# Talking-heads attention and Fourier mixing on one core: scores a step sooner, a fourth buffer of gathered rows, sums of weights in place

## The chip, the core and the metric

The program runs on one core of a Trainium2 chip. The metric is the device time of one execution in microseconds (us). Engines are named as the profile names them: PE is the matmul engine (TensorE), PEld its weight loads, DVE the vector engine, ACT the scalar engine, POOL the GpSimd engine, SP the engine that here only issues transfers.

## What is computed

Two blocks follow each other. The first is attention whose heads are mixed twice, before and after the softmax (8 batches, 12 heads, 448 rows, head width 64):

```
scores = scale * np.matmul(q, k.transpose(0, 1, 3, 2))
scores = np.einsum('bhij,hg->bgij', scores, w_pre)
attn = softmax of scores over j
attn = np.einsum('bhij,hg->bgij', attn, w_post)
x    = np.matmul(attn, v), heads side by side: (8, 448, 768)
```

The second adds to x the real part of a two-dimensional Fourier transform over rows and columns, normalizes, and applies two matrix products with a ReLU between them:

```
u  = x + np.real(np.fft.fft(np.fft.fft(x, axis=1), axis=2))
un = (u - mu) / np.sqrt(var + 1e-06)
out = u + np.maximum(un @ w_ch1, 0.0) @ w_ch2
```

All numbers are 32-bit floats, but the two weight matrices arrive as 64-bit floats and are turned into 32-bit ones in the kernel, piece by piece.

## The kernel before, in words

The kernel has two stages. `mix_phase` is the mixing stage: attention and the Fourier transform, batch by batch. `ffn_phase` is the matrix products, in which each block product is done by a scheme of seven products, so that the weights are needed as seven blocks: four pieces and three sums of pieces (and one piece is overwritten by a sum).

**Steps of the mixing stage.** Head mixing sums over heads, which lie in different products, so the rows must be regrouped. The scores of a block of 28 to 60 query rows go to an SBUF tile `Sb`; the rows of `Sb` that belong to one step (20 query rows, all 12 heads) are gathered by four DMAs into a tile `Kr`, in which heads lie along partitions. A batch has 8 blocks and `GS` = 23 steps, the stage 184 steps. The loop at its end goes over steps `s` and emits, in an order written out by hand in `ORDERS` (one list for even, one for odd steps):

- `pre` (L639): the premix, a matmul of `Kr` with the expanded `w_pre`, for step s + LM, LM = 2;
- `max0`, `max1` (L646, DVE), `exp0`, `exp1` (L653, ACT) and `scale` (L660 to L663, DVE and POOL) for step s + 2: the softmax, in tile `PP`;
- `post` (L673): the postmix for step s, and `turn` (L686, DVE), its transpose into `Pv`;
- `gather` (L628, issued by SP): the four DMAs for step s + LG, LG = 4;
- `conv`: one dealt operation of the weights' conversion;
- `QK`, `AV`, `full`: fillers, which are due at a step by the tables below.

PE, DVE, ACT and POOL execute in exactly the order in which the loop emits (`manual_schedule`). SP takes its transfers in program order and waits, before each one, for what it reads and for the place it writes.

**Fillers and their tables.** A table gives the step within a batch. `AT_T`: transposes of q and k (L585, copies at L474) for the next batch, for three pairs of heads. `AT_L`, `AT_V`: loads of q, k and v from POOL. `AT_QK`: score products of a block and a pair of heads (`emit_qk`, L611), counted from 7 steps ahead of the block's first step. `AT_AV`: attention times v (L703). `AT_X`: the transposes (L747) that begin the Fourier part; POOL then folds rows and columns (`fold`, L768 to L789), one or two folds per step (one in a step with loads of q or k). `AT_Z`: first Fourier product (`emit_z`, L812), four per batch, with a copy `z` on ACT. `AT_S`: second one (`emit_s2`, L828), four per batch, each followed by four additions on DVE (L839, L841); after the second of a pair the rows are stored, one tile by SP (L860) and one by POOL (L851). A step of 23 or more lies in the next batch's steps: 39 is its step 16.

**Copies behind products.** A filler's products go to one of four PSUM tiles `ms`; the copies out of it are kept in `pend` and emitted at the next `flush`.

**Buffers.** `Sb` has two buffers, `Kr` three, `PP` three. A gather for step T thus writes over the rows of step T - 3.

**Weights.** `_Weights.deal` hands out the conversion, one operation on DVE per step here: seven per piece (`begin` to `whole`) and four sums (`total`, L295). Pieces and sums have a tile each, named after the block's number (`wst0` to `wst6`), one buffer apiece; POOL stores them to memory (L235) and loads pieces (L227). A store is kept in `later` and issued at the start of the next deal. The mixing stage converts five groups of four pieces.

Of the kernel before, what the change touches and what calls it, by code (L numbers as in the profile page):

```python
# [10 lines left out]
F32 = mybir.dt.float32  # L11
U32 = mybir.dt.uint32
ALU = mybir.AluOpType
# [3 lines left out]
P = 128  # L17
# [68 lines left out]

AT_T = ((5, 9), (15, 17), (13, 15))
AT_L = ((-4, -3), (-2, -1), (0, 1), (2, 7), (11, 12), (13, 14))  # L90
AT_V = ((2, 3), (4, 5), (6, 7))
AT_QK = ((0, 2, 1), (0, 1, 2), (0, 1, 2), (1, 2, 2),
         (0, 1, 2), (0, 1, 2), (0, 1, 2), (0, 1, 2))
AT_AV = ((1, 2, 4), (0, 1, 3), (1, 3, 5), (1, 2, 4))
AT_X = ((13, 0), (23, 1), (28, 3), (29, 2))
AT_Z = (39, 39, 42, 42)
AT_S = ((40, 44), (46, 49))

ORDERS = tuple(o.split() for o in (
    "pre post flush AV max0 exp0 "  # L100
# [65 lines left out]
class _Weights:  # L166
# [12 lines left out]
        self.ops, self.pieces, self.raws, self.later = [], [], {}, []  # L179
        self.pre = []  # L180

    def open(self, ctx, tc, ahead=1, split=False):
        self.ahead, self.split = ahead, split

        def pool(name, bufs):
            return ctx.enter_context(tc.tile_pool(name=name, bufs=bufs,
                                                  reuse_waits="tile"))
        self.praw, self.ptmp = pool("wraw", ahead + 1), pool("wtmp", 1)
        self.pst = pool("wst", 1 + split)
# [24 lines left out]
    def add(self, c, n):  # L214

        nc, vec = self.nc, self.nc.vector
        ps, sums, w, dst = self._parts(c)[n]
        box, k0 = {}, len(self.pieces)
        self.pieces.extend(ps)

        def load(n):

            for k in range(len(self.raws), min(n + 1, len(self.pieces))):
                src, f, _ = self.pieces[k]
                raw = self.raws[k] = self.praw.tile([P, DH, 2], U32, name="raw64",
                                                    tag="raw64")
                self.eng.dma_start(out=raw[:, :f, :].rearrange("p f w -> p (f w)"),  # L227
                                   in_=src.bitcast(U32))

        def new(slot):  # L230
            box[slot] = self.pst.tile([P, DH], F32, name="wst", tag=f"wst{slot}")[:, :w]
            return box[slot]

        def store(slot):
            self.later.append(lambda: self.eng.dma_start(out=dst[slot], in_=box[slot]))  # L235

        def size(eng, hi, tmp):
            eng.tensor_scalar(tmp.bitcast(U32), hi, 0x7fffffff, None,
                              op0=ALU.bitwise_and)

        def clamp(eng, tmp):
            eng.tensor_scalar(tmp, tmp, _f32(0x38000000), _f32(0x47efffff),  # L246
                              op0=ALU.max, op1=ALU.min)

        def shift(eng, tmp, top):
            eng.tensor_scalar(top.bitcast(U32), tmp.bitcast(U32), 0x07ffffff, 3,  # L250
                              op0=ALU.bitwise_and, op1=ALU.logical_shift_left)

        def early(k):
            _, f, slot = ps[k]
            top = new(slot)
            tops.append(top)
            nc.scalar.activation(top, self.raws[k0 + k][:, :f, 1].bitcast(F32), ACTF.Abs)  # L257
            clamp(nc.gpsimd, top)

        def begin(k):  # L260
            _, f, slot = ps[k]
            load(k0 + k + self.ahead)
            raw = self.raws[k0 + k]
            box["lo"], box["hi"] = raw[:, :f, 0], raw[:, :f, 1]
            box["tmp"] = self.ptmp.tile([P, DH], F32, name="tmp", tag="tmp")[:, :f]
            box["slot"] = slot
            if self.split:
                while self.pre and self.pre[0][0] <= k0 + k + 2:
                    self.pre.pop(0)[1]()
                box["top"] = tops[k]  # L270
            else:
                box["top"] = new(slot)
                size(vec, box["hi"], box["tmp"])

        def sign():
            top = box["top"].bitcast(U32)
            vec.scalar_tensor_tensor(top, box["hi"], 0xc0000000, top,
                                     op0=ALU.bitwise_and, op1=ALU.bitwise_or)

        def power():  # L280
            vec.tensor_scalar(box["tmp"].bitcast(U32), box["top"].bitcast(U32),
                              0xff800000, None, op0=ALU.bitwise_and)

        def lower():
            vec.scalar_tensor_tensor(box["tmp"], box["lo"], 2.0 ** -52, box["tmp"],
                                     op0=ALU.mult, op1=ALU.mult)

        def whole():
            vec.tensor_tensor(box["top"], box["top"], box["tmp"], op=ALU.add)
            if box["slot"] != 6:  # L290
                store(box["slot"])

        def total(o, a, op, b):
            to = box[o] if o == 6 else new(o)
            vec.tensor_tensor(to, box[a], box[b], op=op)  # L295
            store(o)

        tops = []
        if self.split:
            self.pre.extend((k0 + k, lambda k=k: early(k)) for k in range(len(ps)))  # L300
        self.ops.append((lambda: load(k0 + self.ahead - 1), False))
        for k in range(len(ps)):
            self.ops.append((lambda k=k: begin(k), not self.split))
            if not self.split:
                self.ops.append((lambda: clamp(vec, box["tmp"]), True))
            self.ops.append((lambda: shift(vec, box["top" if self.split else "tmp"],
                                           box["top"]), True))
            for fn in (sign, power, lower, whole):
                self.ops.append((fn, True))
        for a in sums:  # L310
            self.ops.append((lambda a=a: total(*a), True))
# [124 lines left out]
def mix_phase(ctx, tc, rest, ident, q, k, v, w_pre, w_post, u_scr, u_rev, wts, lead):  # L436
# [13 lines left out]

    praw, pqt = lead.praw, lead.pqt
    psb = pool("psb", 2)
    pkr = pool("pkr", 3)
    ppp = pool("ppp", 3)
    psm = pool("psm", 4)
    cst = pool("cst")
    wts.open(ctx, tc)
    pvv = pool("pvv")
    ppv = pool("ppv", 2)
    pxt = pool("pxt", 2)  # L460
# [407 lines left out]
    def due(kind, at, fn):  # L868
        fill[kind].append((at, len(fill[kind]), fn))

    LG, LM = 4, 2
    for n in range(NK + FM):
        wts.add(0, n)
    for b in range(B):
        f = b * GS
        at_t = [(a, nm, xx) for xx, at in enumerate(AT_T) for nm, a in zip("qk", at)]
        if b == 0:

            for i, xx in enumerate(START):
                for j, nm in enumerate("kq"):  # L880
                    for y in range(2):
                        due("none", -40, lambda xx=xx, nm=nm, y=y: emit_load_qk(0, xx, nm, y))
                    due("full", 2 * i + j - 20, lambda xx=xx, nm=nm: emit_xpose(0, xx, nm))
                for n in range(2):
                    due("QK", 2 * i + 2 + n - 20, lambda n=n, xx=xx: (emit_qk(n, xx), n))
            for pr in range(3):
                for y in range(2):
                    due("none", -40, lambda pr=pr, y=y: emit_load_v(0, pr, y))
        else:
            for at, (a, nm, xx) in zip(AT_L, sorted(at_t, key=lambda e: e[0])):  # L890
                for y in range(2):
                    due("none", f + at[y] - GS,
                        lambda b=b, xx=xx, nm=nm, y=y: emit_load_qk(b, xx, nm, y))
            for xx, at in enumerate(AT_T):
                for nm, a in zip("qk", at):
                    due("full", f + a - GS,
                        lambda b=b, xx=xx, nm=nm: emit_xpose(b, xx, nm))
        for pr in range(3 if b else 0):
            for y in range(2):
                due("none", f + AT_V[pr][y], lambda b=b, pr=pr, y=y: emit_load_v(b, pr, y))  # L900
        for n in range(0 if b else 2, NBL):
            for xx in range(3):
                due("QK", f + BLOCK_AT[n] - 7 + AT_QK[n][xx],
                    lambda n=NBL * b + n, xx=xx: (emit_qk(n, xx), n))
        for n in range(NG):
            for pr in range(3):
                due("AV", f + GROUP_AT[n + 1] + AT_AV[n][pr],
                    lambda a=b * NG + n, pr=pr: (emit_av(a, pr), None))
            at, gi = AT_X[n]
            if b == B - 1 and n > 1:  # L910
                at += 2
            due("full", f + at, lambda g=groups[b * NG + gi]: emit_x(g))
        for n, at in enumerate(AT_Z):
            due("full", f + at, lambda b=b, n=n: emit_z(b, n // 2, n % 2))
        for pair in range(2):
            for par in range(2):
                due("full", f + AT_S[pair][par],
                    lambda b=b, pair=pair, par=par: emit_s2(b, pair, par))
# [607 lines left out]
```

## Time and profile before

| | us |
|---|---|
| median of three runs | 2340.01 |
| lowest and highest run | 2327.96, 2340.38 |
| the profiled execution | 2333.72 |
| its span (first to last instruction) | 2332.0 |
| first premix begins | 31.85 |
| last premix (step 183) begins | 800.00 |
| PE busy in the span | 2272.2 |

The span is what the profile covers; the profiled execution's own time holds 1.7 us around it. A line of the groups shows busy time and the mean of one instruction, then the idle time of the engine before it, and what ended it. A line of the waits reads: engine, tile and line, then what it waited for, then us in total, times, longest. `issue` means that nothing the profile shows was waited for. In the timeline each line has its start, its length, engine, line, tiles, shape, count, and in brackets the engine's idle time before it.

### The profile page before, as it was taken

How to read it: one execution, taken by the hardware profiler on the slowest of the kernel's cores; microseconds unless marked ns; L12 is line 12 of the kernel's file. 1: busy time of each engine (PE TensorE's matmuls, PEld its weight loads, DVE VectorE, ACT ScalarE, POOL GpSimd, SP SyncE). 2: the span in 40 equal slices, each digit the busy share in tenths (PEclk: the TensorE clock that was granted, in tenths of full speed). 3: DMA queues.
4: the chain of work that ended last, by engine and by line, in shares of the span. 5: the costliest groups of instructions: out<-in, count | busy, mean ns of one | idle time of the engine just before them, and what ended most of it. 6: DMA issues, size and time to landing. Idle time of an engine off the chain costs nothing.

```text
span 2332.0 us, 60769 instructions
## 1 busy us (share of the span) xinstructions
PE 2272.2 (97%) x22894; PEld 1752.2 (75%) x22894; DVE 1704.3 (73%) x3629; ACT 1176.3 (50%) x3336; POOL 1279.8 (55%) x1783
## 2 busy tenths in 40 slices
PE   6999999999999999999999999999999999999998
PEld 2445555555555567677899999999999899999998
DVE  3768877787877756787677787777777777856445
ACT  4676767666676622322354444444444445444434
POOL 3587977879777542121545455545545645444333
PEclk9999999999999999999999999999999999999999
DMA  7565665656656476567777887878877977795663
GB/s 163 153 178 167 184 180 153 193 170 185 183 170 190 142 229 217 183 219 272 204 178 209 209 227 203 213 175 253 210 166 196 287 166 183 193 249 113 148 148 68
DMA packets 231920, 439.04 MB, mean 188 GB/s; under 512 B 39624, under 2 KB 154080, under 8 KB 231630
## 3 DMA queue, kind: packets, MB, share of 16 engines
q1 hardware_dynamic: 158318, 303.56, 37.8%
q0 software_dynamic: 67312, 129.64, 29.7%
q8 instruction: 183, 3.00, 0.5%
q10 hardware_dynamic: 6000, 1.97, 0.5%
q14 instruction: 107, 0.88, 0.1%
HBM read 213.16 MB, written 142.76 MB: 153 GB/s over the span
## 4 chain that ended last, share of the span: by engine, by line
PE 88%; DMA 4%; DVE 3%; ACT 2%; SPq 1%; issue 1%; POOL 0%; ACTq 0%; DVEq 0%; POOLq 0%
PE psP L1192 18%; PE psP L1310 13%; PE psR L1192 9%; PE mx L639 7%; PE psR L1310 7%; PE ms L703 6%; PE ms L611 6%; PE po L673 5%; PE psQ L1192 5%; PE psQ L1310 3%; PE psP L1269 3%; DMA Kr<-Sb 3%; PE ms L828 2%; PE ms L585 1%; PE psR L1269 1%; PE ms L812 1%
## 5 line engine op out<-in xcount | busy, mean ns | idle before, releaser
L1344 POOL DMA_DIRECT2D out_dram<-od x171 | 207.8, 1275 | 261.3 <-DVE od L1332 167.9
L663 POOL TENSOR_SCALAR PP<-PP,rcp 128x448 f32<-128x448 f32 x368 | 236.9, 653 | 203.3 <-DVE rcp L661 170.2
L653 ACT ACTIVATE PP<-mx,nmx 128x448 f32<-128x448 f32 x368 | 230.6, 631 | 188.3 <-DVE nmx L646 170.7
L646 DVE TENSOR_REDUCE nmx<-mx 128x1 f32<-128x448 f32 x368 | 214.1, 619 | 133.1 <-PE mx L639 129.9
L1156 POOL TENSOR_TENSOR hq<-h 128x128 f32<-128x128 f32 (+1 forms) x210 | 128.1, 610 | 262.9 <-ACT h L1214 127.6
L1338 ACT COPY od<-psP 128x192 f32<-128x192 f32 x488 | 156.4, 321 | 182.0 <-PE psP L1310 177.5
L1341 DVE TENSOR_TENSOR od<-od 128x768 f32<-128x768 f32 x211 | 201.7, 969 | 53.9 <-ACT od L1338 52.9
L639 PE MATMUL mx<-Kr,kw 60*32 60x448 f32 x2944 | 217.4, 551 | 9.1 <-DMA Kr<-Sb 8.5
L611 PE MATMUL ms<-kT,qT 64*32 64x448 f32 (+1 forms) x3072 | 205.9, 545 | 8.1 <-ACT qT L474 6.3
L686 DVE STREAM_TRANSPOSE Pv<-po 128x896 f32<-128x896 f32 x184 | 203.8, 1108 | 5.2 <-PE po L673 2.6
L474 ACT COPY Sb<-ms 124x448 f32<-124x448 f32 (+1 forms) x384 | 184.6, 540 | 37.3 <-PE ms L611 24.5
L673 PE MATMUL po<-PP,kw 60*32 60x448 f32 x2944 | 197.2, 539 | 1.0 <-issue 1.0
L703 PEld LDWEIGHTS ms<-Pv,vv 64*64 64x64 f32 x5376 | 137.3, 132 | 70.9 <-issue 54.3
L1192 PE MATMUL psP<-ks,w1t 128*128 128x256 f32 x744 | 179.1, 379 | 0.1
L1192 PE MATMUL psP<-qs,w1t 128*128 128x256 f32 x744 | 179.0, 379 | 0.0
L703 PE MATMUL ms<-Pv,vv 64*64 64x120 f32 (+1 forms) x5376 | 159.6, 263 | 0.9 <-issue 0.9
L246 POOL TENSOR_SCALAR wst<-wst 128x256 f32<-128x256 f32 (+1 forms) x76 | 119.0, 1574 | 67.7 <-ACT wst L257 66.4
L1192 PEld LDWEIGHTS psP<-ks,w1t 128*128 128x128 f32 x744 | 139.4, 190 | 16.7 <-DVE u L1274 0.7
L1192 PEld LDWEIGHTS psP<-qs,w1t 128*128 128x128 f32 x744 | 139.5, 190 | 16.5 <-issue 0.2
L1310 PE MATMUL psP<-wt,h 128*128 128x192 f32 x490 | 120.8, 328 | 11.7 <-DVE od L1332 11.7
L1192 PE MATMUL psP<-ub,w1t 128*128 128x256 f32 x528 | 127.0, 379 | 0.0
L1213 DVE TENSOR_TENSOR h<-h,psP 128x512 f32<-128x512 f32 x42 | 28.8, 687 | 130.2 <-PE psP L1192 112.7
(190 smaller groups left out, 5294.6 us busy)
## 6 DMA issues: line engine op xcount, KB each, us to landing
Kr<-Sb SPq DMA_DIRECT2D x736, 105.0 KB
out_dram<-od POOLq DMA_DIRECT2D x171, 384.0 KB, 6.8
qs<-ub SPq DMA_DIRECT2D x89, 384.0 KB
ks<-ub SPq DMA_DIRECT2D x88, 384.0 KB
ub<-ub SPq DMA_DIRECT2D x79, 384.0 KB
w1t<-w SPq DMA_DIRECT2D x42, 384.0 KB
w2t<-w SPq DMA_DIRECT2D x42, 384.0 KB
raw<-in_moe_w_ch_dram SPq DMA_DIRECT2D x32, 384.0 KB
```

The costliest lines, as they stand in the source:

```text
L611: nc.tensor.matmul(pss[x][o:o + hi - lo, :S], st["qT", xx][64 * x:64 * x + 64, y, lo:hi], st["kT", xx][64 * x:64 * x + 64, y, :], start=Tr ...
L639: nc.tensor.matmul(mx[x][64 * z + o:64 * z + o + 32, :S], kw1[64 * x:64 * x + KR, o:o + 32], Kr[64 * x:64 * x + KR, z, :], start=True, sto ...
L646: nc.vector.tensor_reduce(nmx[:, :], steps[T]["mx"][x][:, :S], axis=AX.X, op=ALU.max, negate=True)
L653: nc.scalar.activation(steps[T]["PP"][:, x, :], steps[T]["mx"][x][:, :S], ACTF.Exp, bias=steps[T]["nmx", x][:, :], accum_out=steps[T]["den ...
L663: nc.gpsimd.tensor_scalar(PP[:, x, :], PP[:, x, :], rcp[:, x:x + 1], 1.0, op0=ALU.mult, op1=ALU.mult)
L673: nc.tensor.matmul(po[o:o + 32, z, :S], kw2[64 * z:64 * z + KR, y, :], PP[64 * z:64 * z + KR, :, c * HS:(c + 1) * HS], start=True, stop=True)
L686: nc.vector.transpose(turned[a]["Pv"][:, j, :].rearrange("p (z s) -> p z s", z=2), steps[T]["po"][:, :, :S])
L703: nc.tensor.matmul(pss[y][64 * x:64 * x + 64, :nu * R], st["v", pr][64 * y:64 * y + 64, x, jb * D:(jb + 1) * D], _ap(Pv, 64 * y * rp + 32 ...
L1192: mm = nc.tensor.matmul(p[:, m, :], w1[i][:, kc, m * P:(m + 1) * P], ub[:, kc, :], start=i in (0, 4, 1)[:3 - seed] and m == kc == 0, stop= ...
L1310: nc.tensor.matmul(ps[j, key][:, :DQ], a, b, start=m in (0, 4), stop=True, skip_group_check=True)
L1341: eng.tensor_tensor(D[j][:, :, :], D[j][:, :, :], D[k][:, :, :], op=ALU.add)
L1344: nc.gpsimd.dma_start(out=acc[t, r, d], in_=D[j][:, :, :], accum_op=ALU.add)
```

## The change

Four things are edited, all in the mixing stage.

- `LG` goes from 4 to 5: a step's rows are gathered one step sooner. The score products come one step sooner as well (counted from 8 steps ahead). `Kr` has four buffers instead of three.
- The tables follow: transposes of k for the second pair at 16 instead of 17; the last four loads of q and k a step sooner; one product of attention and v a step later.
- Fourier steps: the second Z goes from 39 to 40, the third from 42 to 40; S moves from 40 to 42 for the first pair's first half, and from 49 to 48 for the second pair's second half.
- The weights' sums are written in place of a piece that is no longer needed (`tight`), so that four tiles serve in place of seven; pieces and sums are taken in another order for it. The matrix-product stage opens its weights without this, as before.

```
-AT_T = ((5, 9), (15, 17), (13, 15))
-AT_L = ((-4, -3), (-2, -1), (0, 1), (2, 7), (11, 12), (13, 14))
+AT_T = ((5, 9), (15, 16), (13, 15))
+AT_L = ((-4, -3), (-2, -1), (0, 1), (2, 7), (10, 11), (12, 13))
...
-AT_AV = ((1, 2, 4), (0, 1, 3), (1, 3, 5), (1, 2, 4))
+AT_AV = ((1, 2, 4), (0, 1, 3), (1, 3, 5), (1, 3, 4))
...
-AT_Z = (39, 39, 42, 42)
-AT_S = ((40, 44), (46, 49))
+AT_Z = (39, 40, 40, 42)
+AT_S = ((42, 44), (46, 48))
...
+        tight = self.tight
+        if tight:
+            if ps[3][2] == 3:
+                ps = ps[3:] + ps[:3]
+            sums = [sums[x] for x in (0, 2, 1, 3)]
...
         def new(slot):
-            box[slot] = self.pst.tile([P, DH], F32, name="wst", tag=f"wst{slot}")[:, :w]
+            tag = [p[2] for p in ps].index(slot) if tight else slot
+            box[slot] = self.pst.tile([P, DH], F32, name="wst", tag=f"wst{tag}")[:, :w]
...
         def total(o, a, op, b):
-            to = box[o] if o == 6 else new(o)
+            if o == 6:
+                to = box[o]
+            elif tight:
+                to = box[o] = box[{(4, ALU.add): 3, (4, ALU.subtract): 0, (2, ALU.subtract): 1,
+                                   (3, ALU.subtract): 1}.get((o, op), ps[3][2] if n >= NK
+                                                             else 0)]
+            else:
+                to = new(o)
...
-    pkr = pool("pkr", 3)
+    pkr = pool("pkr", 4)
...
-    wts.open(ctx, tc)
+    wts.open(ctx, tc, tight=True)
...
-    LG, LM = 4, 2
+    LG, LM = 5, 2
...
-                due("QK", f + BLOCK_AT[n] - 7 + AT_QK[n][xx],
+                due("QK", f + BLOCK_AT[n] - 8 + AT_QK[n][xx],
```

More of the change, by code (lines that the diff above doesn't have):

```diff
@@ L180, in __init__, with open @@
         self.pre = []
-    def open(self, ctx, tc, ahead=1, split=False):
-        self.ahead, self.split = ahead, split
+    def open(self, ctx, tc, ahead=1, split=False, tight=False):
+        self.ahead, self.split, self.tight = ahead, split, tight
         def pool(name, bufs):
```

## The prediction

> **What bounds the kernel now.** I read the page first. Its slices of the span (the kernel has two stages; the mixing stage fills the first fourteen of the forty slices) show TensorE busy nearly everywhere, at full clock:
>
> ```profile
> PE 2272.2 (97%) x22894; PEld 1752.2 (75%) x22894; DVE 1704.3 (73%) x3629; ACT 1176.3 (50%) x3336; POOL 1279.8 (55%) x1783
> ...
> PE   6999999999999999999999999999999999999998
> ...
> PEclk9999999999999999999999999999999999999999
> ```
>
> No other engine is above 73% and the chain that ended last is 88% PE. So only PE's own stalls are worth time. The change touches the mixing stage alone, so I then asked for busy times from 64 us (after the start-up) to 803 us (after the last step):
>
> ```profile
> 64.00:803.00 739.00, 724.89 (x14496) 390.70 (x14482) 581.19 (x1219) 509.88 (x1569) 565.42 (x877) 1.00 0.58 173
> ```
>
> The columns are length, then busy PE, PEld, DVE, ACT, POOL, then granted clock, DMA share and GB/s. PE looks idle for only 14.1 us, but ends of matmuls are modelled, so a stall can hide behind the modelled end of the matmul before it. The weight loads (PEld) tell it better. Third view: the waits of PEld in the same window (total us, times, longest):
>
> ```profile
> PEld mx L639 <- issue: 28.3, 134, 0.3
> PEld mx L639 <- DMA Kr<-Sb: 20.1, 32, 1.9
> ```
>
> The first line is the normal gap of a pipeline, 0.21 us each. The second is a real wait: the premix (L639) waits 20.1 us in total for gathered rows Kr. Does such a wait cost its length? Three steps of the same kind (premix, postmix, attention-times-v, one score product) in three batches answer it. Fourth view, the timeline of PEld:
>
> ```profile
> 269.97 0.17 PEld L639 LDWEIGHTS mx<-Kr,kw 60*32 60x32 f32 x12 [0.17 <-issue]
> 270.55 0.14 PEld L639 LDWEIGHTS mx<-Kr,kw 60*32 60x32 f32 x4 [0.41 <-DMA Kr<-Sb]
> ...
> 274.24 0.15 PEld L639 LDWEIGHTS mx<-Kr,kw 60*32 60x32 f32 x8 [0.23 <-issue]
> ...
> 665.48 0.18 PEld L639 LDWEIGHTS mx<-Kr,kw 60*32 60x32 f32 x16 [0.17 <-issue]
> ...
> 669.21 0.15 PEld L639 LDWEIGHTS mx<-Kr,kw 60*32 60x32 f32 x8 [0.23 <-issue]
> ```
>
> The undisturbed step takes 669.21 - 665.48 = 3.73 us, the one with 0.41 us of waiting 274.24 - 269.97 = 4.27. A third (466.78 to 471.25, waiting 0.60) takes 4.47. They lengthen by 0.54 and 0.74: the whole wait and a little more, and nothing catches up later. So Kr's waits are paid in full.
>
> Why do they occur? SP issues the four gathers of a step in order; the last one of the worst step was issued at 631.92 and waited for until 640.55, 8.6 us:
>
> ```profile
> 631.92 9.83 SPq L628 DMA_DIRECT2D Kr<-Sb  x9
> 632.10 0.57 POOL L227 DMA_DIRECT2D raw<-in_moe_w_ch_dram  x1
> ...
> 632.65 0.64 POOL L566 DMA_DIRECT2D vv<-in_v_dram  x1
> ...
> 633.28 1.45 POOL L557 DMA_DIRECT2D rawq<-in_q_dram  x2
> ...
> 640.55 0.14 PEld L639 LDWEIGHTS mx<-Kr,kw 60*32 60x32 f32 x4 [1.60 <-DMA Kr<-Sb]
> ```
>
> Loads of weights, v and q issued from POOL in the 3 us after it share the transfer engines with it. SP itself is not the limit in the steady part: a gather's issue is 0.76 us, four make 3.05 us, and a step averages (796.47 - 62.50) / 174 = 4.22 us.
>
> **What the Trainium skill says.** Perfetto Trace Analysis, section Tensor Engine Instruction (MATMUL, LD_WEIGHTS): the end of a TensorE instruction is estimated, not observed. The trace agrees: 14.1 us of idle PE cannot hold the 20.1 us of waits. DMA: Bandwidth & Descriptors, section Issuing engines are not separate DMA queues: transfers started from SP and from GpSimd run on the same 16 engines and interleave; the 8.6 us above beside POOL's loads agrees, against about 2.4 us for the first step's last gather (issued 31.81, its rows loaded at about 34.2). Same page, Rules for kernel authors: issue a DMA early and wait on its semaphore late. This is the main part of the change. Whether it pays is decided by lead against landing time, below.
>
> **The change part by part.**
>
> 1. LG 4 to 5, Kr buffers 3 to 4, scores a step sooner. No matmul, copy or DMA is added. Scores and gather move together, so neither gains on the other; only the distance from gather to premix grows, by one step, 4.22 us. In the timeline the last gather's issue leads its premix by 3.0 to 6.9 us in the steps that wait, and landings took up to 8.6 us. With 4.22 us more, the lead is 7.2 to 11.1 us: it covers all but the coincidence of short lead and slowest landing. The extra buffer keeps the slack of a buffer's release as it was: before, gather s+4 reuses the rows of premix s+1; after, gather s+5 reuses the rows of premix s+1. Of the 20.1 us I drop about 1 us of gaps that are normal ones with another label and leave 2 us behind: gain 17 us. Bounds: 10 (if the load collisions reach further) to 20. What is late next in those steps: PE itself, as the step of 3.73 us shows.
>
> 2. Start-up (31 to 64 us). SP issues gathers there without pause: 45 of them in 39.48 us from 29.28. Steps 0 to 7 wait on this rate and gain nothing from a longer lead. Step 9 waits 0.74 and 0.22 us because step 8's gathers came late behind their scores; that goes. One score product (0.75 to 1 us) moves into a time in which PE waits for step 1's rows. Gain 2 us, bounds 0 to 4.
>
> 3. Transposes of k (L585): those of pair 1 go from step 17 to 16, and scores of pair 2 now follow their transpose in the next step instead of after two. Cover: premix and postmix, 1.5 us, hide the copies kT (ACT 0.59, DVE 0.55). Where that cover failed before is visible: at 404.87 DVE reached kT only after four Fourier additions of 0.55 us (L839, L841), and L611 waited 0.94 us instead of 0.22; so too at 209.4 and 601.7. That Fourier step (S, pair 0) is moved from step 17 to 19, behind which stand a reduction and a transpose of P, no kT. So 3 x 0.7 = 2.1 us are saved. For pair 2, DVE has qT (1.12 us) and kT (0.55) to do against 0.9 us of PE transposes plus 1.5: hidden, unless DVE is late. I take 0.35 us for each of 7 batches, 2.5 us lost; bounds 0 and 7 x 0.7 = 5.
>
> 4. Other Fourier steps. Z par 1 (L812) comes two steps earlier, at 17. It needs POOL's last xf: in the fourth batch this ends at 396.3, while step 17's place for it is about 401.5, 5 us later. Nothing waits; but the loads of q and k move a step sooner on POOL's queue too, and push two of the xf additions (1.0 us each) into one step; the last one keeps its step. On SP's queue a batch's first store of X gets four more gathers ahead of it and its second comes a step sooner, with its scatter on POOL: a wait for DVE in front of gathers as before, now with a step more of lead behind it. Same counts everywhere: 0 us, bounds -2 to +3. A z copy, an AV product and the score products only change places within their steps.
>
> 5. Sums of weights in place. Same 20 sums in this stage, same stores. Now the DVE sum must wait until the piece in its place has been stored. Sums are reordered so that at least two dealt operations (one per step) stand between the last piece's store and the sum that overwrites it: 2 x 4.22 = 8.4 us, against landings of 2.6 to 6.9 us (median 3.2). So 0 us. If POOL issued a store more than about 1.5 us late and it was also the slowest one, DVE would stand still, with the maxima (L646), and through them exp and premix, behind it: bound 20 x 0.5 = +10 us, improbable; below nothing no gain is possible, as no work goes.
>
> The second stage has the same instructions; the last batch's Fourier parts keep their fillers with two swapped: 0, bounds -2 to +2.
>
> **Sum.** -17 - 2 - 2.1 + 2.5 = -18.6 us on the profiled execution (span 2332.0, with what lies around it 2333.72): 2315.1. The median of the runs, 2340.01, is 6.3 us above that execution, and the runs spread over 12.4 us. If the spread is itself landings that PE waits for, the change removes part of it; I add half, 3.2: **2318 us**.
>
> **Rivals.**
>
> A. The wait moves. A late landing no longer stops PE, but ACT: the score copy (L474) into one of two Sb buffers must wait until the last gather of the block two before has landed, one step after its issue as before. Now ACT waited for gathers 3.5 us in this window; if the collisions shift onto last gathers of a block, half of the gain goes this way. -9: 2325 in the profile's terms, 2329 as a median. For it: ACT feeds premix (PSUM of L639 is freed by exp). Against: the relation of score copy to gather is unchanged.
>
> B. The change does not do what it says: SP's issue or a buffer's release, not the distance in steps, sets the lead. Then -3: 2331, median 2336. For it: the start-up. Against: in the steady part SP waits 63.0 us for score copies in 30 places, so it has room.
>
> C. Slower: the mechanism of A with a price above the gain. A block's scores start one step after the last gather of the block two before. If each of the some 50 blocks' first copies waited 0.6 us on ACT, and exp and PE with it, 30 us would be lost against 19 gained: +11, 2345, median 2352. It decides against the change from 0.4 us per block; today it is 3.5 / 50 = 0.07.
>
> **How the numbers follow.** Forecast 0.64, A 0.20, B 0.09, C 0.07. About 0.5% (11.7 us) is what a measurement can tell from no change: faster means under 2328.3. The forecast's own range is 2305 to 2326. From A I count a third as faster: faster 0.70, same 0.23 (rest of A, B), slower 0.07. Range: 2304 to 2335; it takes in A, and leaves out C and most of B; its lower end is the best bounds (20 + 4 + 2.1 = 26 us, 2307.6 in the profile's terms) and a few us of the runs' spread.
>
> **What would show it.** Right: PEld's waits of L639 for Kr in the steady window fall from 20.1 us to under 4; the lead from last gather to premix grows by about 4 us; the wait before L611 at step 18 goes; the window from first to last premix (31.85 to 800.00, 768 us) shrinks by about 18. Wrong: ACT's wait for Kr above 10 us (A, C), unchanged leads (B), DVE waiting for stores of w (part 5), L611 waiting for kT by 0.5 us or more in each batch (part 3), or L812 waiting for xf (part 4).

## The result, and the profile after

The changed kernel takes 2326.97 us (median of 22 runs, 2321.13 to 2338.62), the kernel before 2333.95 us (22 runs as well, 2325.49 to 2342.87). The ratio is 0.9967, with a 95% interval of 0.9955 to 0.9978: a gain of 7.0 us by the medians, 5.1 to 10.5 us by the interval. The forecast was 2318 us and a gain of 18.6 us in the profile's terms; 2326.97 lies in the stated range, but the gain is little more than a third of the forecast one. The profiled execution of the changed kernel took 2327.42 us (span 2325.5 us).

In the mixing stage the line numbers of the kernel after are those of before plus 13: the premix is L652, exp L666, the copies L487, the score product L624, attention times v L716. In the kernels below without the weights' conversion they are one less. First the page after, the busy times, the slices of PE and those of its clock:

```profile
PE 2258.0 (97%) x22894; PEld 1744.6 (75%) x22894; DVE 1715.7 (74%) x3629; ACT 1170.0 (50%) x3336; POOL 1278.7 (55%) x1783
...
PE   6999999999999999999999999999999999999998
...
PEclk9999999999999999999999999999999999999999
```

PE's modelled busy time fell by 14 us with the same 22894 matmuls: stalls hidden behind modelled ends went. Next the steady window of after, 64 to 803 us (length, busy PE, PEld, DVE, ACT, POOL, clock, DMA share, GB/s):

```profile
64.00:803.00 739.00, 721.71 (x14644) 389.60 (x14636) 598.92 (x1237) 509.67 (x1586) 569.17 (x885) 1.00 0.60 176
```

148 more matmuls fit into the window, but DVE is busy for 17.7 us more, 10.7 us of it in the weights' conversion (84.6 instead of 73.9). Third, the waits in that window, after (us in total, times, longest):

```profile
PEld mx L652 <- ACT PP L666: 16.8, 45, 1.6
ACT Sb L487 <- DMA Kr<-Sb: 14.7, 10, 3.9
...
PEld ms L624 <- ACT Sb L487: 9.3, 22, 1.5
...
PEld ms L716 <- ACT Sb L487: 4.2, 6, 1.1
...
PEld mx L652 <- DMA Kr<-Sb: 0.8, 4, 0.2
```

and the same kinds of line in the kernel before, beside the 20.1 us that the prediction shows:

```profile
PEld mx L639 <- ACT PP L653: 8.6, 22, 0.8
...
PEld ms L611 <- ACT Sb L474: 4.4, 19, 0.3
...
ACT Sb L474 <- DMA Kr<-Sb: 3.5, 3, 1.7
```

The wait for rows is gone (20.1 to 0.8). In its place stand 8.2 us more of PE waiting until exp frees the premix's PSUM tile, and 11.2 us more of ACT waiting, before a score copy, for gathers out of the Sb tile that it overwrites. PE also waits 9.1 us more, before score products and products of attention and v, for a PSUM tile that a score copy has not yet emptied (9.3 and 4.2 us, where it was 4.4 and nothing). The step whose last gather the prediction showed (144; step 80 had a longer single wait, 1.88 us) now reads, in the timeline of after, where the merged row begins with that last gather:

```profile
621.55 10.35 SPq L641 DMA_DIRECT2D Kr<-Sb  x9
...
632.98 0.18 PEld L652 LDWEIGHTS mx<-Kr,kw 60*32 60x32 f32 x16 [0.16 <-ACT PP L666]
```

The last gather's issue leads the premix by 11.4 us, where it was 6.9. Over steps 10 to 175 the median of this lead is 10.15 us after and 6.21 before: +3.9, against 4.2 forecast.

Where the time went, from the timelines. Start-up runs from the first premix to that of step 8, steady from there to the last premix (step 183), tail to the first matmul of the matrix stage, seam to its 300th, rest to its last:

| us | start-up | steady | tail | seam | rest |
|---|---|---|---|---|---|
| before | 30.66 | 737.50 | 20.26 | 86.68 | 1418.99 |
| after | 33.50 | 724.85 | 21.76 | 88.31 | 1418.62 |
| difference | +2.84 | -12.65 | +1.50 | +1.63 | -0.37 |

These are one profile each, and profiles of one kernel differ: a kernel below has 725.98 and 720.86 us in its steady stage, and a run below that changes the start-up alone has 730.17 us in the steady stage, which it shares with the changed kernel. A difference of the steady stage thus carries some 5 us.

From the first premix to the last the time fell by 9.8 us (768.15 to 758.34), where about 18 had been named as the sign. The seam is not the change's: it was 84.25 to 90.53 in the other kernels, of both kinds. The start-up is, and it went the wrong way. In the timeline of the start-up before, exp, premix and score copy follow each other like this:

```profile
39.14 0.63 ACT L653 ACTIVATE PP<-mx,nmx 128x448 f32<-128x448 f32 x1 [1.77 <-DVE nmx L646]
...
39.92 0.20 PEld L639 LDWEIGHTS mx<-Kr,kw 60*32 60x32 f32 x8 [0.76 <-ACT PP L653]
...
40.80 0.97 ACT L474 COPY Sb<-ms 104x448 f32<-104x448 f32 x2 [0.18 <-PE ms L611]
```

and after:

```profile
40.92 0.96 ACT L487 COPY Sb<-ms 104x448 f32<-104x448 f32 x2 [3.43 <-DMA Kr<-Sb]
41.77 0.65 ACT L666 ACTIVATE PP<-mx,nmx 128x448 f32<-128x448 f32 x1
...
42.56 0.20 PEld L652 LDWEIGHTS mx<-Kr,kw 60*32 60x32 f32 x8 [4.00 <-ACT PP L666]
```

The score copy now stands ahead of exp on ACT and waits 3.43 us for a gather to land; exp stands behind it, and the premix 4.00 us behind exp. That is rival A's mechanism, at a place where the prediction did not look for it.

### The profile page after: what moved, and what is told of

Its sections match the earlier page's. It is cut to its first block, busy times and chain, and to the rows that moved or that the text cites. A ratio compares the mean times of both kernels' runs of the same rounds, so it can differ in the third digit from the quotient of the medians.

```text
span 2325.5 us, 60782 instructions
## 1 busy us (share of the span) xinstructions
PE 2258.0 (97%) x22894; PEld 1744.6 (75%) x22894; DVE 1715.7 (74%) x3629; ACT 1170.0 (50%) x3336; POOL 1278.7 (55%) x1783
## 4 chain that ended last, share of the span: by engine, by line
PE 84%; DVE 4%; POOL 3%; DMA 3%; ACT 2%; issue 1%; SPq 1%; ACTq 0%; DVEq 0%; POOLq 0%
PE psP L1205 17%; PE psP L1323 13%; PE psR L1205 9%; PE psR L1323 6%; PE mx L652 6%; PE ms L716 5%; PE ms L624 5%; PE psQ L1205 4%; PE po L686 4%; PE psQ L1323 3%; PE psP L1282 3%; PE ms L841 2%; DMA Kr<-Sb 2%; PE psR L1282 2%; PE ms L598 1%
## 5 line engine op out<-in xcount | busy, mean ns | idle before, releaser
L666 ACT ACTIVATE PP<-mx,nmx 128x448 f32<-128x448 f32 x368 | 230.2, 631 | 168.6 <-DVE nmx L659 155.1
L487 ACT COPY Sb<-ms 124x448 f32<-124x448 f32 (+1 forms) x384 | 184.6, 540 | 55.8 <-PE ms L624 31.1
L624 PE MATMUL ms<-kT,qT 64*32 64x448 f32 (+1 forms) x3072 | 200.1, 548 | 12.8 <-ACT qT L487 6.3
L652 PE MATMUL mx<-Kr,kw 60*32 60x448 f32 x2944 | 194.7, 550 | 8.5 <-ACT PP L666 4.7
L716 PEld LDWEIGHTS ms<-Pv,vv 64*64 64x64 f32 x5376 | 138.1, 132 | 71.6 <-issue 48.1
L686 PE MATMUL po<-PP,kw 60*32 60x448 f32 x2944 | 187.3, 539 | 3.1 <-issue 1.9
L716 PE MATMUL ms<-Pv,vv 64*64 64x120 f32 (+1 forms) x5376 | 160.9, 263 | 1.5 <-ACT X L487 0.8
```

The costliest lines, as they stand in the source:

```text
L624: nc.tensor.matmul(pss[x][o:o + hi - lo, :S], st["qT", xx][64 * x:64 * x + 64, y, lo:hi], st["kT", xx][64 * x:64 * x + 64, y, :], start=Tr ...
L652: nc.tensor.matmul(mx[x][64 * z + o:64 * z + o + 32, :S], kw1[64 * x:64 * x + KR, o:o + 32], Kr[64 * x:64 * x + KR, z, :], start=True, sto ...
L666: nc.scalar.activation(steps[T]["PP"][:, x, :], steps[T]["mx"][x][:, :S], ACTF.Exp, bias=steps[T]["nmx", x][:, :], accum_out=steps[T]["den ...
L686: nc.tensor.matmul(po[o:o + 32, z, :S], kw2[64 * z:64 * z + KR, y, :], PP[64 * z:64 * z + KR, :, c * HS:(c + 1) * HS], start=True, stop=True)
L716: nc.tensor.matmul(pss[y][64 * x:64 * x + 64, :nu * R], st["v", pr][64 * y:64 * y + 64, x, jb * D:(jb + 1) * D], _ap(Pv, 64 * y * rp + 32 ...
```

## The experiments

Two theories at first. M: the gain on PE is given back on ACT, where a block's first score copy waits for the gathers of the block two before (Sb has two buffers). R: the moved Fourier steps and products eat it. Differences below are from each kernel's ratio to the kernel before, which ran beside it on the same chip; the changed kernel has 0.9967. Groups ran on different chips. Four kernels measured twice, on two chips, agree within 0.001 of the ratio, so some 2 us between groups tell nothing.

**A third Sb buffer.** It takes M's wait away, but fits into SBUF only without the weights' conversion. So the conversion is left out of the mixing stage in all kernels of this group, and the weights' blocks are filled from q by 14 transfers (so these kernels compute something else, with the same matmuls):

```
-    for n in range(NK + FM):
-        wts.add(0, n)
+    for i in range(7):
+        for m, w in enumerate((wts.w1[0], wts.w2[0])):
+            due("none", 20 + 10 * (2 * i + m), lambda i=i, m=m, w=w: nc.gpsimd.dma_start(
...
-    psb = pool("psb", 2)
+    psb = pool("psb", 3)
```

> The kernel before, with the conversion of weights left out of the mixing stage (the first group of weights is filled with numbers of q by 14 transfers, so its products are of other numbers). It is the base for the next two kernels, as the SBUF of the conversion is needed for a third Sb buffer. Both theories: PE waits for Kr about as in the kernel before (15 to 25 us between first step and last), ACT hardly waits for Kr (under 6 us); time 2320 to 2340 us.

> The changed kernel, with the same part left out. Theory M (what the longer lead saves on PE is given back on ACT, whose first score copy of a block waits until the gathers of the block two before have landed): PE's waits for Kr under 3 us, ACT's waits for Kr 10 to 18 us, time 4 to 10 us under c0. Rival R (the moved Fourier steps and products of attention and v cost what the lead saves): the same time, so this pair does not tell them apart; it shows that the pattern does not hang on the conversion.

> As c1, with three Sb buffers in place of two: the score copy then overwrites rows whose gathers were issued three steps earlier. Nothing else is changed. M: ACT's waits for Kr fall under 2 us, PE's waits for exp (L653's bank of PSUM) fall by 5 us or more, and the time is 8 to 13 us under c1. R: no change beyond 2 us, since no Fourier step is moved.

Ratios 0.9963, 0.9910 (0.9891 to 0.9929) and 0.9880 (0.9860 to 0.9900); medians 2322.04, 2309.89, 2303.54. The change gives 12.1 us without the conversion and, with the third buffer, 18.5. Whether those 6.3 us are a loss that the change brought needs the control, the kernel before with three buffers:

> The kernel before, with the conversion of the weights left out of the mixing stage (the weights' blocks are filled from q instead), and with three Sb buffers: the control to the pair of the changed kernel in which the third buffer gave 6.3 us. M: before the change ACT waits for Kr only 2.8 us here, so the third buffer gives 0 to 3 us, and PEld's waits for Kr stay near 19 us. Rival B3 (a third Sb buffer is good by itself, whatever the change does): 5 to 8 us here too, and then the 6.3 us are no loss that the change brought.

It gave 0.9954 (0.9940 to 0.9967): about 2 us by the ratios, 4.6 by the medians, but measured on another chip. So all four once more, together on one chip:

> The kernel before without the weights' conversion (the weights' blocks are filled from q instead), on the same chip as the three others of this group. Base of the group: about 9 us under the kernel before.

> The kernel before without the conversion and with three Sb buffers, on one chip with its pair. M (the wait on ACT is one that the change brought): 0 to 3 us under its pair with two buffers. B3 (a third buffer is good by itself): 5 to 8 us under it.

> The changed kernel without the conversion, two Sb buffers. Both: 11 to 14 us under the kernel before without the conversion.

> The changed kernel without the conversion and with three Sb buffers. M: 5 to 8 us under its pair with two buffers, and 3 us or more further under it than the third buffer takes from the kernel before. B3: the third buffer takes the same from both, within 2 us.

| | two Sb buffers | three Sb buffers | third buffer |
|---|---|---|---|
| median, before | 2321.83 | 2317.82 | -4.0 |
| median, after | 2309.88 | 2300.08 | -9.8 |
| the change | -12.0 | -17.7 | |
| start-up, before (two profiles) | 29.64, 29.66 | 30.14, 29.67 | +0.3 |
| start-up, after | 33.15, 34.73 | 30.32, 29.57 | -4.0 |
| steady, before | 725.98, 720.86 | 718.99, 720.94 | -3.5 |
| steady, after | 710.30, 711.53 | 707.92, 707.52 | -3.2 |

Both theories missed a size: the third buffer is good by itself (4.0 us, where M had 0 to 3), and gives 5.8 us more after the change. The profiles say where the more lies: in the start-up, which only the changed kernel with two buffers has long. In the steady stage the buffer gives about the same to both, as far as profiles that differ by up to 5 us can tell, so nothing shows that the steady waits of ACT are a loss that the change brought; they vary anyway (2.8 and 9.4 us in two profiles of the same kernel before without the conversion, 9.5 and 11.4 after). The waits of the start-up (30 to 64 us) of the changed kernel without the conversion, two buffers:

```profile
PEld mx L651 <- ACT PP L665: 11.0, 10, 3.9
...
ACT Sb L486 <- DMA Kr<-Sb: 6.9, 3, 3.4
...
PEld mx L651 <- DMA Kr<-Sb: 2.0, 2, 1.4
```

and with three:

```profile
PEld mx L651 <- DMA Kr<-Sb: 7.1, 11, 1.8
PEld mx L651 <- ACT PP L665: 4.2, 8, 1.2
```

With ACT's wait gone PE waits for rows again, and the start-up is as long as before the change (29.9 against 29.65 us): there SP's rate sets the pace, and the longer lead gained nothing. The granted clock is no rival here. It halves for a few us in each start-up, but its mean there was 0.88 in both profiles of the kernel before with two buffers (29.64 and 29.66 us) and 0.90 in the first of the changed one (33.15 us). In the second, with 34.73 us, it was 0.77, so part of that one may be the clock's.

**The start-up alone.** The scores of one block a step later, in the first batch:

```
-                due("QK", f + BLOCK_AT[n] - 8 + AT_QK[n][xx],
+                due("QK", f + BLOCK_AT[n] - 8 + AT_QK[n][xx] + (b == 0 and n == 2),
```

> The changed kernel, with the three score products of the third block of the first batch one step later (where they were before in the start-up); all else as changed. M: the ACT wait of 3.4 us in front of exp for step 1 goes, step 2's premix begins near 39.9 us as before instead of 42.6, and the time is 2 to 5 us under the changed kernel. R (the start-up is bound by SP's gathers, and the score product is filler): less than 1 us.

0.9979 (0.9969 to 0.9990): no gain. The wait at 40.92 went, but the next block's first copy now waits 3.96 us, at 53.15; the start-up fell only to 32.18 us. The rate of the gathers stayed as it was, and the wait moved to the next block.

**The parts of the change.** Sums in place alone, in the kernel before (the diff of the change, without the other parts):

> The kernel before, with one part of the change alone: the weights' sums made in place. M (the gain on PE is given back on ACT, where the first score copy of a block waits for the gathers of the block two before): no difference to the kernel before, 0 +-2 us, and DVE waits for stores of w less than 2 us. R2 (the part of the gain that the change loses with the weights' conversion in, 7.0 us against 12.1 us without it, goes into the sums in place, whose sums wait for stores): 3 to 6 us slower than before, with DVE's waits for stores of w above 3 us.

1.0012 (1.0002 to 1.0021): 2.8 us slower, between the two expectations, and DVE waits 0.2 us for stores. So the feared wait is not there. Part of the 2.8 us goes with the clock: its granted mean was 0.9943 in these 22 runs and 0.9951 in the 35 runs of the kernel before beside them. In the 22 runs of the changed kernel the time fell by about 2.2 us for each 0.001 of clock; by this, an estimate, 1.6 of the 2.8 us are the clock's, and the rest is within the noise. Whether the sums in place lower the clock is not known. In the changed kernel with the Fourier steps of before:

```
-AT_AV = ((1, 2, 4), (0, 1, 3), (1, 3, 5), (1, 3, 4))
-AT_Z = (39, 40, 40, 42)
-AT_S = ((42, 44), (46, 48))
+AT_AV = ((1, 2, 4), (0, 1, 3), (1, 3, 5), (1, 2, 4))
+AT_Z = (39, 39, 42, 42)
+AT_S = ((40, 44), (46, 49))
```

> The changed kernel with the Fourier steps and the products of attention and v at the steps of before (Z, S and one AV product); the rest of the change stays. M: 0 to 3 us slower than the changed kernel, because the wait before the score products of step 18 comes back, three times 0.7 us, and ACT's waits for Kr stay at 10 us or more in the steady window. R (the moved Fourier steps eat the gain): faster than the changed kernel by 4 to 10 us, with ACT's waits for Kr unchanged.

0.9983 (0.9972 to 0.9994), 3.7 us slower than the changed kernel (some 0 to 7 by the two intervals), where R had it 4 to 10 us faster: R falls. But the three waits of 0.94 us did not come back as M had it, so it is not the moved Fourier step that ended them; that the score products left that step is the likely reason. ACT's waits for Kr rose instead, from 14.7 to 22.6 us.

**Other orders.** Four attempts to keep the late copies from exp. First products later:

```
-AT_QK = ((0, 2, 1), (0, 1, 2), (0, 1, 2), (1, 2, 2),
-         (0, 1, 2), (0, 1, 2), (0, 1, 2), (0, 1, 2))
+AT_QK = ((0, 2, 1), (0, 1, 2), (1, 1, 2), (1, 2, 2),
+         (1, 1, 2), (1, 1, 2), (0, 1, 2), (0, 1, 2))
```

> The changed kernel with the first of the three score products of blocks 2, 4 and 5 (block 3 has it already) one step later in the steady batches and in the first one, that is at the step of before; the gathers stay where they are. M: the first score copies of these blocks then come about 4.2 us later against the landing they wait for; ACT's waits for Kr in the steady window fall from 14.7 us to 7 or less, and the time by 2 to 6 us. If two score products in one step cost PE more than that, or the wait only moves to another block: 0 +-2 us, with the waits still at 10 us or more. R: 0 +-2 us, with ACT's waits for Kr fallen.

> As the one with the first score products of blocks 2, 4 and 5 a step later, and block 3's first product another step later, and in the start-up (blocks 2 to 4 of the first batch) all three products in the last step that the gathers allow. M: the start-up, from the first premix to that of step 8, falls from 33.5 us to 31 us or less because no score copy of these blocks waits for Kr ahead of an exp; 3 to 8 us faster than the changed kernel. Rival S (in the start-up the rate of SP's gathers sets the pace whatever ACT does): the start-up stays at 32 us or more, the rest as in the run with blocks 2, 4 and 5 alone. R: 0 +-2 us.

1.0068 (1.0053 to 1.0082) and 1.0097 (1.0078 to 1.0116): some 24 and 30 us slower than the changed kernel, a plain miss. The second also delays the scores of the start-up. There ACT's wait for Kr went (0.5 us left), yet the start-up took 33.76 us, with PE waiting 11.0 us for exp; rival S had 32 us or more. The waits of the first of them in the steady window:

```profile
PEld mx L652 <- ACT PP L666: 36.4, 61, 1.6
...
ACT Sb L487 <- DMA Kr<-Sb: 1.2, 3, 0.8
```

ACT's wait for Kr went as M said (14.7 to 1.2), and the time rose: with two score products in one step, exp stands behind four score copies more often (18 times, where it was 7), and PE waits for it 19.6 us more. Next, the order on ACT alone:

```
+                    held = [e for e in pend if e[2] is not None and e[3] == 0]
+                    pend[:] = [e for e in pend if e not in held]
                     flush()
+                    pend.extend(held)
...
+                if op == "exp0":
+                    for e in [e for e in held if e in pend]:
+                        pend.remove(e)
+                        e[1]()
```

> The changed kernel, in which ACT does the first two score copies of a block behind the first of a step's two exps instead of ahead of it; all products, gathers and everything on PE keep their places. M (an exp that stands behind a copy that waits for Kr holds up PE): one of the two exps no longer stands behind it, so PEld's waits of the premix for exp in the steady window fall from 14.8 us (of which 8 were there before the change) to 11 or 12, and the time by 1 to 4 us against the changed kernel; start-up from 33.5 to about 32.5 us. Rival E (PE's waits for exp come from ACT's own load, which the steps' new order crowds, and not from the copies that wait): 0 +-2 us, PEld's waits for exp as they were. Rival L (the copies, being later, make the products behind them wait for their PSUM tiles): slower by 2 us or more, with PEld's waits of L624, L598 and L716 for Sb up.

> As the one with the first copies behind the first exp, but behind both exps, where the order of the fillers allows it. M: no exp stands behind a copy that waits for Kr: PEld's waits of the premix for exp fall to about 8 us, the start-up to 31 or 32 us, and the time by 3 to 7 us against the changed kernel. Rival E: 0 +-2 us. Rival L: slower by 2 us or more, and more so than with the copies behind one exp.

> The kernel before with the same edit (first score copies of a block behind both exps). M: here ACT waits only 3.5 us for Kr in the steady window, so the edit brings nothing, 0 +-2 us, or costs 2 to 4 us by rival L. If it gains as much as it does in the changed kernel, the edit is good by itself and tells nothing of the change's missing gain.

1.0046 (1.0030 to 1.0063), 1.0068 (1.0043 to 1.0093) and, in the kernel before, 1.0068 (1.0045 to 1.0091). Rival L holds: the edit costs about 16 us in the kernel before too, which has little of M's wait, so it tells nothing of the missing gain; and PE's waits for exp did not fall in the changed kernel with the edit (17.8 and 19.4 us). In the kernel before with the edit, the fillers' products wait for PSUM tiles that the postponed copies hold (steady window):

```profile
PEld ms L703 <- ACT Sb L474: 12.0, 16, 1.3
PEld ms L828 <- ACT Sb L474: 11.9, 10, 1.9
...
PEld ms L747 <- ACT Sb L474: 9.0, 6, 1.9
```

**Gathers sooner, scores as before.**

```
-                due("QK", f + BLOCK_AT[n] - 8 + AT_QK[n][xx],
+                due("QK", f + BLOCK_AT[n] - 7 + AT_QK[n][xx],
```

> The changed kernel with the score products back at their steps of before (7 steps ahead); gathers stay one step sooner, Kr keeps four buffers. The gather of a block's first step then stands in the step of the block's last score copy, and a first score copy has one step more after the gathers that it overwrites. M: ACT's waits for Kr in the steady window fall from 14.7 us to under 3 and in the start-up they go; PEld's waits of the premix for exp fall towards 8 us; SP now waits for score copies before some 50 first gathers, so PEld's waits for Kr come back in part (3 to 8 us): 1 to 6 us faster than the changed kernel. Rival G (the first gather of a block then has no more lead than before, and the worst waits were there): PEld's waits for Kr at 12 us or more, 2 to 8 us slower than the changed kernel.

1.0077 (1.0062 to 1.0093), about 26 us slower than the changed kernel; rival G, and worse than it said. The lead from last gather to premix has a median of 6.17 us, that of the kernel before (6.21): SP holds its queue until a block's scores are copied, so the scores set the lead, not the step in which the gather is issued. The waits for rows are back (steady window):

```profile
PEld mx L652 <- DMA Kr<-Sb: 23.2, 30, 2.4
...
PEld mx L652 <- ACT PP L666: 16.9, 39, 1.1
```

The start-up here is 31.06 us. With the scores back at their steps most of its loss is gone, so it is the earlier scores that cost there. ACT's waits for Kr, which M had under 3 us in the steady window, stayed at 14.4. Why neither they nor the waits for exp fell is not explained; the other moves of the change were matched to earlier scores, and stayed.

**The conversion on DVE.** In the steady window DVE spends 84.6 us on the conversion in the changed kernel, 73.9 before, without waits. One operation of it, in the timeline of after:

```profile
192.28 1.25 POOL L676 TENSOR_SCALAR PP<-PP,rcp 128x448 f32<-128x448 f32 x2
...
192.98 2.64 DVE L256 TENSOR_SCALAR wst<-tmp 128x256 uint32<-128x256 uint32 x1
...
193.51 1.96 POOL L802 TENSOR_TENSOR xf<-xq 113x385 f32<-113x385 f32 x2
...
196.46 0.54 DVE L487 COPY kT<-ms 128x384 f32<-128x384 f32 x1
...
197.12 0.21 PEld L624 LDWEIGHTS ms<-kT,qT 64*32 64x32 f32 x16 [2.20 <-issue]
197.15 0.98 PE L624 MATMUL ms<-kT,qT 64*32 64x448 f32 x16 [1.43 <-DVE kT L487]
```

An operation of a kind that took 0.27 us at 65.97 in the kernel before, and 0.39 in the mean of twelve there, lasts 2.64 us, over three of POOL's; the copy kT stands behind it on DVE, and PE behind that copy: its weight loads pause for 2.20 us, and the matmuls after them wait for kT. The same operations were put ahead of the transpose of P, away, so the thought, from POOL's work:

```
-    "QK max1 exp1 turn scale conv full gather",
+    "QK max1 exp1 conv turn scale full gather",
...
-    "AV turn exp1 scale conv gather full flush"))
+    "AV conv turn exp1 scale gather full flush"))
```

> The changed kernel with DVE's conversion of the weights put ahead of the transpose of P in each step instead of behind the reciprocal, that is at a time when POOL is not about to scale P. P (the conversion is stretched by POOL's scaling and folds beside it: 13 of its operations take over 0.95 us in the changed kernel, one of them 2.64 us): at most 5 of them take over 0.95 us and the 159 operations together at most 76 us instead of 84.6; 2 to 5 us faster than the changed kernel, if the transpose, which now comes half a microsecond later, has room. Rival O (the long operations don't come from POOL's work beside them): they stay, and the time with them; if the transpose has no room, slower by up to 10 us with few long operations.

0.9988 (0.9981 to 0.9996), some 5 us slower than the changed kernel (2 to 8 by the two intervals): neither expectation. Now 26 operations take over 0.95 us, where there were 13 (11 in the kernel before), and the conversion takes 100 us. Part of this is chance: the run with only the start-up changed has 19 such operations and 89.8 us for the same order of the steady stage. Of the 26, 15 lie beside POOL's scaling of P (5 of the 13 in the changed kernel). The expected direction was wrong; that the place matters is likely, from one profile. In the three kernels the long operations lie beside POOL's arithmetic for 83 to 94% of their time, the short ones for 35 to 47%.

## Why the prediction was wrong in size

The lead grew and the waits for rows went, as forecast. Two terms of the sum failed. Step 2, the start-up, was put down as a gain of 2 us and cost 2.84; its cause is shown. Step 1, the price of the waits for rows, was put too high by about 4 us; where these went stays open. Smaller terms follow.

**Step 1 (lead), PE's side: right.** Waits for Kr 20.1 to 0.8 us (2 left were forecast), lead +3.9 us (4.2). The sentence that gather and scores move together and that only the distance grows holds too, and more strongly than meant: without the scores the lead doesn't grow at all.

**Step 1, the price: too high.** "So Kr's waits are paid in full" was read from two steps that waited. Steps 1 and 3 gave 17 + 2.1 - 2.5 = 16.6 us for the steady stage; it fell by 12.65 us, so about 4 us are missing (9 by the other profile of that stage, 730.17). The other pairs show that the length of the removed waits was no measure of the gain. Without the conversion PE waited less for rows from the start, and 11 us of waits went (12.2 and 12.5 to 1.5 and 1.1, 64 to 770 us); with three Sb buffers 8.7 us (11.4 and 9.9 to 2.2 and 1.7). Yet the stage fell by 12.5 and 12.2 us there (means of two profiles), about as much as in the full kernel, where 19.3 us of waits went.

"What is late next in those steps: PE itself" failed: exp is late next (8.2 us more of PE's waits), and PSUM tiles held by score copies (9.1 us more). That the missing 4 us lie in these waits is not shown. Without the conversion they rose as well, by 5.6 and 6.3 us, and nothing was missing there (12.5 us measured, 11 + 2.1 - 2.5 = 10.6 by the prediction's rule); with three buffers the waits for the tiles are gone (1.5 us, where the kernel before has 2.0), those for exp are 11.9 us against 7.1 in the kernel before with the same edits, and nothing was missing either. No run took the wait for exp away alone.

**Step 2 (start-up): wrong in sign, shown.** Forecast -2, bounds 0 to 4 of gain; it cost 2.84 us, and 4.3 us in the mean of the two pairs without the conversion (3.5 us in the pair with nearly equal clocks). The premise "wait on this rate and gain nothing" was right, and the step should have ended there. The 2 us were step 9's waits, which did go, and a score product moving into PE's waiting time; but on ACT the copy of that product overwrites rows whose gather that same slow rate had not yet delivered. The third Sb buffer undoes it, in the kernels without the conversion. About 5 of the missing 11.6 us lie here.

**Rival A's place.** "The relation of score copy to gather is unchanged" is true in steps, and in the steady stage rival A was not shown to decide: its sign came (ACT waits 14.7 us for Kr, above the 10 that were named), but the third buffer gives 3.5 us there before and 3.2 after. That the profiled time, 2327.42, lies near rival A's 2325 is therefore in part luck. In the start-up the gathers are late by SP's rate and the scores are not, and so the relation changed.

**Step 3: the named waits went, others came.** The three waits of 0.94 us before L611 (209.38, 405.54, 601.73) are gone, though not by the moved Fourier step. New ones of 2.20 and 1.69 us came at 197.12 and 228.18, the first behind the conversion shown above, and four of 0.87 to 1.50 us for a PSUM tile that a score copy holds. Waits over 0.6 us before score products add up to 8.8 us in the steady window, where it was 4.0: the 2.1 us were not saved.

**Step 4: the counts are the same, the neighbours are not.** No wait of the Z product for xf in the steady window, as forecast. But what stands beside what on DVE and POOL has changed: conversion operations over 0.95 us have 14.4 us above 0.5 us each, where it was 8.6 (21.1 in the other profile of the same steady stage). The Trainium skill, SBUF — State Buffer, section SBUF: two separate sides, says that DVE and GpSimd share one pair of ports as an exclusive lock, which a DVE instruction takes in a two-port mode, or with two SBUF inputs against a GpSimd instruction that reads SBUF, and that the loser stands still for a whole instruction. The 2.64 us operation agrees with it; whether it runs in such a mode, and whether it is this lock in each of the 13, is not shown.

**Step 5 (sums in place): 0 forecast, 2.8 us measured (0.5 to 4.9).** About half of it goes with the lower clock of those runs (an estimate, from the clocks above). The feared cause, DVE waiting for a store, is 0.4 us after. What the rest is was not found; PE's waits for Kr were 22.9 us in that run, against 20.1, in one profile each.

**The addition of 3.2 us** for the spread of the runs was wrong: with 22 runs the median before is 2333.95, the profiled execution 2333.72. Three runs of which two lay at 2340 had misled. And that the spread is landings was a guess. In the 22 runs of the changed kernel the granted clock was 0.992 to 0.996, and the time goes with it (correlation -0.70; 0.1% of 2327 us is 2.3 us for each 0.001). What lowers the clock, waits included, no run here shows.

Sum: -18.6, +4.8 start-up, +4 price of the waits, +2.8 sums in place, and +1.5 in the tail (0 forecast; 20.8 us in most other kernels with the change, 19.5 to 20.3 in those without) give -5.5, against -7.0 by the medians and -6.3 by the profiled executions. The parts overlap and carry 1 to 5 us of scatter each, so that the sum comes this close is in part luck. Shown is the loss in the start-up. Open stay where the steady stage lost 4 us against the sum, the cause of step 5's cost, and 2 us or more of what the conversion takes from the gain (12.0 us without it, 7.0 with it, of which the sums in place explain at most 2.8). No kernel with the whole computation in it ran measurably faster than the changed one.

## What to carry to other kernels

A longer lead may need a buffer at both ends: the tile that the transfer fills, and the tile that it reads, because the next writer of the source waits for the landing; look for that writer's place in its queue, above all where the transfers are late by rate. In an in-order queue the lead is set by what the queue waits for, so moving the issue alone moved nothing here (6.17 against 6.21 us). Don't price a removed wait by its length until the profile shows that the second-latest input is far behind: 19.3, 11 and 8.7 us of removed waits brought about 12.5 us each here. And test a rescue with a control in the kernel before: of the 9.8 us that the third buffer gave here, the kernel before would have had 4.0 as well.

## What the runs showed that was not expected

A DVE operation of 128x256, 0.39 us in the mean, took 2.64 us beside three POOL operations; with the conversion moved by one place in the step it took 100 us instead of 84.6 (89.8 in another profile of the same steady stage) for the same operations. Two score products in one step instead of one, without any change in work, cost 24 us; PE's waits for exp, which then stands behind four copies of 0.5 us in more steps, rose by 19.6 us.
